# A new order for the start of an attention and expert kernel: batch 0's powers in two chains, its weight norm on TensorE, three products in two turns

## The chip, the cores and the metric

The kernel runs on one core of a Trainium2 chip. The metric is the device time of one execution in microseconds, the median of three runs.

## The reference, cut to what matters

Eight batches of Nystrom attention (8 heads, 576 positions, 64 wide, 32 landmarks) feed a layer of 8 experts, of which each token takes one.

```
q_lm, k_lm = means of q, k over 18 positions each        # 32 landmarks
A  = sm(q, k_lm); Bm = sm(q_lm, k_lm); C = sm(q_lm, k)   # softmax of scaled scores
Z  = Bm.T / (norm1(Bm) * norminf(Bm) + 1e-06)            # both norms over the whole batch and head
for _ in range(6): Z = 2 * Z - Z @ Bm @ Z
x  = A @ Z @ C @ v                                       # (B*S, 512)
expert = argmax(normed x @ normed emb.T / tau)
out    = gate * (relu(x @ w1[expert]) @ w2[expert])
```

## The kernel before

Tokens of one batch mostly go to one expert, so the kernel guesses an expert per batch (`guess`, `choose`), loads that expert's two weight matrices, and computes the batch with them. A count of wrong guesses at the end decides whether a general path runs; it does not here.

One batch goes through these generators. `sums` adds the landmark means of k and q (VectorE alone, or GpSimd halves first and VectorE adds the rest). `inverse` makes Bm, its transpose bt, the two norms, and the first residual (tile ek). `powers` does the six Newton steps as powers of the residual: every step multiplies the residual with itself and with the running product, both in one group of matmuls, copies the square and adds the product. `values` takes the scores of landmark queries with all keys, `shifted` and `turned` make their softmax and transpose it (ct), and `weighted` sums the values with it (u). `landmarks` multiplies powers and u (w), transposes that (wt), takes its norm, and prepares the routing weights. `queries` and `scored` make the softmax of all queries against the landmark keys (ae, at, ab). `first_scale` takes the norm of the first expert weights, `first_weights` multiplies wt into them, `scaled` splits the scaled product into two half-precision parts (ww). `first` is the hidden layer (`ab` times `ww`, then `hidden`), `second` the output layer (`w2c` times `ht`, c a chunk of 128 tokens).

All generators are interleaved at build time by `Weave.run`. It reads three tables of characters: TURNS names the generator that takes the next turn, CHOICES picks the engine where a generator offers two, and BANKS the PSUM banks. So the order of the instructions on each engine is fixed in these tables, and each engine works through its list in that order. WARM says before which turn, and how many, 128-column filler matmuls of ones (`keep_warm`) go into TensorE's list.

For batch 0 the norm of the first weights is a sum of squares on ScalarE (L1284), the product with u is transposed on TensorE (L1031), and squared and summed on VectorE (L1040, L1042). The lines that matter in the profile: L587 fillers, L507 all matmuls of the helper `mm`, L858 transposes of ec, L667 landmark sums, L664 and L942 GpSimd's shares, L715 to L757 the norms, L996 to L1000 the powers, L1346 ww, L1385 and L1387 w2c, L1395 and L1397 ht.

Of the kernel before, what the change touches and what calls it, by code (L numbers as in the profile page):

```python
# [19 lines left out]
P = 128  # L20
# [36 lines left out]
    "0c07072o0c0i35073c07073c08073c3d002o003c00080909003d0101010101360101013600003600363g3601363h00340d34340134010d"  # L57
    "34340d34013h3h3g0d0j0j340i0o3n341j1j1j1j1j1j1j1k1j3g013h013g013j3h3g373v3u01010101013i013u0j3i013w3w3w3w3w3w3w"
    "3i3u3w3w3w3v3i3u1l1k1k1k1k3v3w3v1k3u1k0e3w3i3u3w3v3w1l3w001l1k3w3v3u0e0f0f3v3w3w3u3v1l3w3w3w3w3u3u3u3w38383v1l"
    "3v3u1l1n381l3v383k381n1l381l3v3u3838383k383v1n381l383k1n1l1m441m3j1m46461n44461m4547442n2n2n483k3l1n1n3o3m0j45"  # L60
    "1n4702381n3m1n3m3m021n02023m382n2n3m2n382n1n023m1n2n2n38384a024b4c1n2n3l384d49022n2n4e2n4a4b3m2n4f2n482n4g4c49"
    "024d2n4h024e3o0p0p1n4f1n4h4g3l3o1n2n4j1n1n022n4k4k1n2n2o3o4m020o4n4j2n4u2o3m1o1p1o1o1o1o1o1o1p3o022o1o3o4v4v4m"
    "4m1n4v024u4l1p4v024v4m3l4m024l2n4x1n491n2o1p022n4y4i02391p4x024w382o022n39024y022o02501n2o39501q4z4w504z2o3939"
    "1q49030303033p545550035003032o1p4w0303500p54551q032o501q1s2o552o1p504i2o551q1q2o4w031s544o4i03030350032o501q1p"
    "1s5003502o2o54032o4w032o0u540p03501q50031q3a54035054505003541q552o505455551s552o2o3a2o2o2o3a2o592o1s50540k2o1s"
    "55543a593a2o3a502o5559553a3b1s1s5a5a5a505054552o5a1s503q3q3q5a3b3b5a2o3q552o3b1s5a3b5d5d5d1s3q0u5a2o5d3q5d3q5a"
    "5d5a5d5d5a5d5d2o5a3q0k0l5d58583q522o3q542o5a5a3q1s1s1q1s5a3q2o3q5a5a5a525a1s1s585m1r5o5n3b2o5a5n2o525b5b1s3q2o"
    "2o2o2o2o2o2o1s2o2q5o5a1s3q5a1s5n2p2p5a2p2p5o5m3q1s5s5q4o0v2p5b5p5q2p0l5p2p1s2p0v5t5s2q4o5u1s5m4o5t2p5z2p2q5p5w"
    "4o4o605u2p623b5z2p2p5y5w631s2p645y62605y602p5y63613q1061605f2p640404045x615x655y652q603r3r3r3r2q5x04102p6d6d04"
# [400 lines left out]
def nystrom_moe(ctx: ExitStack, tc: tile.TileContext, qT, kT, v, emb, w1, w2, out):  # L470
# [86 lines left out]
    invw = cst.tile([P, B], F32, name="invw")  # L557

    ge = cst.tile([P, B], F32, name="ge")
    gi = cst.tile([P, B], I32, name="gi")  # L560
# [1022 lines left out]
```

## Time and profile before

| | us |
|---|---|
| median of 3 runs | 425.93 |
| lowest, highest | 424.93, 426.79 |
| profiled execution, its own time | 424.86 |
| its span | 423.1 |
| TensorE, VectorE, ScalarE, GpSimd busy | 408.1, 323.5, 258.4, 72.2 |

The span is what the profile shows of one execution; 1.8 us of its time lie around it. In the rows an instruction has its start, its length, its line, and what goes out and in; in brackets stands how long the engine was idle before it, and what it waited for. Lengths of neighbours overlap a little, so the distance between two starts is what an instruction takes up.

### The profile page before, as it was taken

The numbers are of one execution on the slowest core, as the hardware profiler recorded it, in microseconds if no ns is written. First come the engines' busy times: TensorE is split into PE (matmuls) and PEld (weight loads), VectorE is DVE, ScalarE is ACT, GpSimd is POOL, SyncE is SP. The second block draws the span as 40 slices with busy tenths as digits, with TensorE's granted clock in tenths as the row PEclk, the third lists the DMA queues.
The fourth block names the chain that finished last, engine by engine and source line by source line (L and its number), as shares of the span: only waits on it lengthen the run. The fifth ranks groups of instructions, "written<-read, shape, count | busy, mean of one in ns | idle before, by whom it ended". The sixth has DMA issues, their size and how long they took to land.

```text
span 423.1 us, 14672 instructions
## 1 busy us (share of the span) xinstructions
PE 408.1 (96%) x6109; PEld 246.5 (58%) x6109; DVE 323.5 (76%) x1018; ACT 258.4 (61%) x564; POOL 72.2 (17%) x72
## 2 busy tenths in 40 slices
PE   7998999999999999999899999999999999999995
PEld 2543665566644567555575476556665576457644
DVE  4888898989799599986994889947994687668400
ACT  1367579567636985675379747963559548774211
POOL 4133213401233103301222013010320010000000
PEclk9999799999999999999999999999999999999999
DMA  8996079026368937944657239503078218321011
GB/s 298 394 398 210 2 276 384 30 77 203 119 214 309 379 120 238 341 162 142 226 155 288 108 142 359 193 29 107 16 238 324 96 44 319 109 107 51 15 64 57
DMA packets 29850, 77.68 MB, mean 184 GB/s; under 512 B 2768, under 2 KB 14288, under 8 KB 27984
## 3 DMA queue, kind: packets, MB, share of 16 engines
q1 hardware_dynamic: 29488, 76.49, 51.1%
q8 instruction: 49, 0.80, 0.8%
q10 hardware_dynamic: 288, 0.18, 0.2%
q14 instruction: 25, 0.20, 0.2%
HBM read 61.92 MB, written 14.75 MB: 181 GB/s over the span
## 4 chain that ended last, share of the span: by engine, by line
PE 76%; DVE 15%; ACT 5%; issue 2%; DMA 1%; SPq 0%; ACTq 0%; DVEq 0%
PE ps L507 71%; PE ps L587 3%; DVE ht L1397 3%; DVE w2c L1387 2%; DMA q_t<-qT 1%; PE ps L858 1%; ACT junk L1284 1%; DVE qsum L667 1%; DVE cm L804 1%; DVE ae L908 1%; ACT junk L1156 1%; ACT junk L1360 1%; DVE am L915 1%; DVE at L927 1%; DVE asum L921 1%
## 5 line engine op out<-in xcount | busy, mean ns | idle before, releaser
L507 PE MATMUL ps<-w2c,ht 128*128 128x512 f16 (+2 forms) x1176 | 203.6, 341 | 0.6 <-DVE yt L1486 0.6
L507 PEld LDWEIGHTS <-ht 128*128 128x128 f16 (+1 forms) x1176 | 93.2, 102 | 76.5 <-issue 4.5
L507 PE MATMUL ps<-ab,ww 128*128 128x288 f16 x768 | 105.0, 291 | 2.2 <-DVE ww L1346 1.0
L507 PEld LDWEIGHTS <-ww 128*128 128x128 f16 x768 | 74.9, 100 | 30.9 <-issue 4.7
L1395 ACT ACTIVATE ht<-ps 128x288 f16<-128x288 f32 x128 | 50.6, 409 | 53.7 <-PE ps L507 53.0
L1397 DVE SCALAR_TENSOR_TENSOR ht<-ps,ht 128x288 f16<-128x288 f32 x128 | 54.7, 446 | 7.6 <-ACT ht L1395 7.2
L1387 DVE SCALAR_TENSOR_TENSOR w2c<-wstage,wsc,w2c 128x1024 f16<-128x1024 f32 x32 | 41.9, 1309 | 3.4 <-ACT w2c L1385 3.3
L1488 ACT ACTIVATE yt<-ps,gfac 128x512 f32<-128x512 f32 (+1 forms) x34 | 21.5, 634 | 33.3 <-PE ps L507 31.3
L1284 ACT ACTIVATE junk<-wstage 128x1024 bf16<-128x1024 f32 x32 | 33.8, 1056 | 3.4 <-DMA wstage<-w 2.9
L1360 ACT ACTIVATE junk<-wstage 128x1024 bf16<-128x1024 f32 x32 | 33.8, 1055 | 0.7
L1156 ACT ACTIVATE junk<-ps 128x512 bf16<-128x512 f32 (+1 forms) x40 | 23.8, 596 | 15.3 <-DVE lg L1153 13.0
L942 POOL TENSOR_TENSOR ae<-ae,am 128x576 f32<-128x576 f32 x15 | 18.2, 1221 | 77.5 <-DVE am L915 57.8
L1174 POOL TENSOR_TENSOR nrm<-ssq,half 128x5 f32<-128x5 f32 x8 | 9.7, 1208 | 109.9 <-ACT junk L1156 109.9
L587 PE MATMUL ps<-ones 128*128 128x512 bf16 (+3 forms) x90 | 24.2, 405 | 1.7 <-POOL ones L525 1.7
L1153 DVE TENSOR_REDUCE lg<-ps 128x8 f32<-128x64 f32 (+1 forms) x40 | 8.8, 220 | 18.1 <-ACT junk L1156 10.9
L1385 ACT ACTIVATE w2c<-wstage,wsc 128x1024 f16<-128x1024 f32 x19 | 21.7, 1143 | 1.3 <-PE ps L507 1.3
L1346 DVE SCALAR_TENSOR_TENSOR ww<-ps,wsc,ww 128x1024 f16<-128x1024 f32 (+1 forms) x18 | 20.6, 1159 | 1.6 <-ACT ww L1344 1.5
L664 POOL TENSOR_TENSOR half<-k_t 128x576 f32<-128x576 f32 x10 | 13.0, 1297 | 46.7 <-DMA k_t<-kT 24.1
L942 POOL TENSOR_TENSOR ae<-ae,asum 128x576 f32<-128x576 f32 x12 | 13.9, 1160 | 38.2 <-DVE asum L780 24.2
L664 POOL TENSOR_TENSOR half<-q_t 128x576 f32<-128x576 f32 x10 | 14.0, 1404 | 34.2 <-DMA q_t<-qT 15.3
L507 PEld LDWEIGHTS ps<-ek 32*32 32x32 f32 x768 | 12.0, 104 | 12.6 <-DVE ek L1000 4.0
L507 PE MATMUL ps<-ek 32*32 32x64 f32 (+1 forms) x768 | 17.6, 214 | 1.4 <-issue 0.7
(209 smaller groups left out, 524.1 us busy)
## 6 DMA issues: line engine op xcount, KB each, us to landing
wstage<-w SPq DMA_DIRECT2D x64, 512.0 KB, 8.0
v<-v SPq DMA_DIRECT2D x16, 512.0 KB, 7.4
k_t<-kT SPq DMA_DIRECT2D x7, 1152.0 KB, 6.6
q_t<-qT SPq DMA_DIRECT2D x7, 1152.0 KB, 6.6
out<-yt SPq DMA_DIRECT2D x31, 256.0 KB, 3.9
abs__127<-ab SPq DMA_DIRECT2D x8, 576.0 KB, 5.3
k_t<-kT SPq DMA_DIRECT2D x2, 576.0 KB, 4.1
q_t<-qT SPq DMA_DIRECT2D x2, 576.0 KB, 6.6
```

Of the source, the lines that this page charges most:

```text
L507: pe.matmul(o, lhsT, rhs, start=start, stop=stop)
L587: pe.matmul(warmth[:, 0:k * P], ones16, bc(ones16.unsqueeze(1), [P, k, P]), start=True, stop=True)
L664: pool.tensor_tensor(out=half, in0=sv[:, :, :, 0:9], in1=sv[:, :, :, 9:18], op=ALU.add)
L942: pool.tensor_tensor(out=x, in0=x, in1=z, op=op)
L1156: act.activation(junk[lo:hi, 0:512].rearrange("p (j g x) -> p j g x", j=4, g=2), pfv[lo:hi, :, n, :, 0:D], AF.Square, accum_out=ssq[lo:hi, ...
L1284: act.activation(junk, stage[1, b, q], AF.Square, accum_out=sq[:, q:q + 1])
L1360: act.activation(junk, stage[2, b, q], AF.Abs, accum_out=sq[:, q:q + 1])
L1385: act.activation(w[:, 0], st, AF.Copy, scale=sc)
L1387: vec.scalar_tensor_tensor(out=w[:, 1], in0=st, scalar=sc, in1=w[:, 0], op0=ALU.mult, op1=ALU.subtract)
L1395: act.activation(ht[:, 0, r], ph[:, 0:HS], AF.Relu)
L1397: vec.scalar_tensor_tensor(out=ht[:, 1, r], in0=ph[:, 0:HS], scalar=0.0, in1=ht[:, 0, r], op0=ALU.max, op1=ALU.subtract)
L1488: act.activation(yt[:, 0:n], py[:, cols], AF.Copy, scale=fac)
```

## The change

1. `first_scale` for batch 0 multiplies each 128-column block of the weights (their upper halves, read as bf16) with itself on TensorE, adds all 32 products in one bank, and takes the diagonal by one fused VectorE instruction.
2. `powers` for batch 0 becomes two generators: `squares` (TensorE, then one copy) and `products` (TensorE, then one addition on VectorE), so that the squares do not wait for the additions.
3. `landmarks` for batch 0 gets the transposed product by a second group of matmuls instead of a transpose; its norm is one fused VectorE instruction on the transposed tile (`bound`).
4. `values`, `queries` and `weighted` are two turns each, and of `values` each half's maximum may start when its half is done.
5. `inverse`: the larger row sum is the product of the softmax sum and its reciprocal, and the sign of the residual is carried into the first addition. The scale of the first weights is made of the bits of both norms at once, with one reciprocal.
6. `second_weights` may take its sums on VectorE.
7. Small tiles have more buffers, and TURNS, CHOICES, BANKS and WARM are new. The description of the change says of the new order that GpSimd may hold VectorE up in it.

```
 TURNS, CHOICES, BANKS: new strings
-WARM = {18: 69, 26: 35, 47: 9, 52: 28, 60: 2, 89: 20, 103: 30, 107: 12, ... 204: 3}      # 18 entries
+WARM = {17: 53, 22: 68, 27: 3, 32: 10, 50: 8, 52: 1, 66: 1, 77: 9, ... 203: 11, 208: 13} # 20 entries
 def inverse(bs):
-        vec.tensor_reduce(ntv[:, 1], bm, axis=AX.X, op=ALU.add, apply_absolute_value=True)
+        vec.tensor_tensor(out=ntv[:, 1], in0=bs4, in1=br4, op=ALU.mult)
...
-        wv.add(powers(bs, t))
+        if bs == (0,):
+            ts = [t]
+            wv.add(squares(ts))
+            wv.add(products(ts))
+        else:
+            wv.add(powers(bs, t))
+    def squares(ts):
+        for k in range(5):
+            pz, done = yield from take(T(170, 32, cols=64, tiles="blocks"), 1)
...
+                    mm(pzv[r, g], ts[k][r, 0, 1, g], ts[k][r, 0, 1, g])
+            yield "get", "ek"
+            ts.append(residual(1))
...
+            if (yield "any", (("act", 115), ("dve", 135))) == "act":
+                act.copy(ts[k + 1][:, 0, 1], pzv)
...
+    def products(ts):
+        for k in range(6):
+            if k:
+                yield "wait", ("r", k)
...
+                    mm(pzv[r, g], ts[k][r, 0, 1, g], ts[k][r, 0, 0, g])
...
+            vec.tensor_tensor(out=ts[k + 1][:, 0, 0], in0=ts[k][:, 0, 0], in1=pzv, op=ALU.add if k else ALU.subtract)
+    def bound(b, sq, *tiles):
+        if b == 0:
+            vec.tensor_tensor_reduce(ws2, *tiles, *tiles, 1.0, 1e-30, ALU.mult, ALU.add, sq)
+            pf, put = yield from take(T(130, 4, cols=4), 1)
+            f2 = pf[:, 0:1]
+            mm(f2, ones, sq)
+        else:
+            f2, put = yield from total(sq, 1)
+        vec.tensor_scalar(hbw[:, b:b + 1], f2.bitcast(I32), 1, EXP_MASK, op0=ALU.logical_shift_right,
+                          op1=ALU.bitwise_and)
...
 def landmarks(b):
+        if b == 0:
+            quads[b] = yield from take(T(150, 32, cols=128, tiles="halves"), QUAD, "quad")
+            pwt = quads[b][0][:, :, 512 - M:512]
...
+                    mm(pwt[64 * g:64 * g + 64, j], u0[b][r, g], x0[b][r, g])
...
+            wv.add(bound(b, sq, wt_))
 def first_scale(b):
+        if b == 0:
+            work, pg = T(700, 16, cols=1024), None
+            for q in range(4):
...
+                lead = stage[1, b, q].bitcast(BF16).rearrange("p (x i) -> p x i", i=2)[:, :, 1]
+                for i in range(8):
+                    x = lead[:, P * i:P * i + P]
+                    mm(pg[:, 0:P], x, x, start=(q == i == 0), stop=(q == 3 and i == 7))
...
+            vec.tensor_tensor_reduce(ws3, pg[:, 0:P], ident, 1.0, 1e-30, ALU.mult, ALU.add, sq1)
...
+        yield "wait", ("hbw", b)
+        vec.tensor_scalar(sc, hbw[:, b:b + 1].bitcast(F32), 2.0 ** 58, inv1[:, b:b + 1], op0=ALU.mult, op1=ALU.mult)
         yield V(20)
-        vec.reciprocal(sc, inv1[:, b:b + 1])
-        yield "wait", ("scw", b)
-        vec.tensor_scalar(sc, sc, scw[:, b:b + 1], None, op0=ALU.mult)
+        vec.reciprocal(sc, sc)
 def second_weights(b):
-            act.activation(junk, stage[2, b, q], AF.Abs, accum_out=sq[:, q:q + 1])
+            if (yield "any", (("act", 1056), ("dve", 1135))) == "act":
+                act.activation(junk, stage[2, b, q], AF.Abs, accum_out=sq[:, q:q + 1])
+            else:
+                vec.tensor_reduce(sq[:, q:q + 1], stage[2, b, q], axis=AX.X, op=ALU.add, apply_absolute_value=True)
```

VectorE, batch 0's norms (bt is Bm's transpose, nts the sums, nm their maxima, cc their product's reciprocal). Before:

```order
L735 TENSOR_REDUCE nts_116<-bt 128x2
L738 STREAM_TRANSPOSE ntt<-nts_116 128x64
L741 TENSOR_REDUCE nm<-ntt 128x2
L667 TENSOR_REDUCE ksum<-k_t 128x64
L744 TENSOR_SCALAR cc<-nm 128x1
L746 RECIPROCAL cc<-cc 128x1
L749 TENSOR_SCALAR ccb<-cc 128x32
```

and now:

```order
L741 STREAM_TRANSPOSE ntt<-nts_117 128x64
L744 TENSOR_REDUCE nm<-ntt 128x2
L747 TENSOR_SCALAR cc<-nm 128x1
L615 RECIPROCAL con<-con 128x1
L749 RECIPROCAL cc<-cc 128x1
L752 COPY ccb<-cc 128x32
```

The landmark sum of the next batch's keys (ksum) no longer stands inside the norms.

VectorE, batch 0's six additions of the powers (ek). Now, from the first to the last, with all that stands between them:

```order
L929 TENSOR_REDUCE am<-ae 128x18
L1030 TENSOR_TENSOR ek<-ek,ps 128x64
L669 TENSOR_REDUCE qsum<-half 128x64
L842 TENSOR_TENSOR cfac<-cfac,rct 128x2
L958 TENSOR_TENSOR ae<-ae,am 128x576
L935 TENSOR_REDUCE asum<-ae 128x18
L669 TENSOR_REDUCE ksum<-k_t 128x64
L783 TENSOR_SCALAR asum<-asum 128x18
L785 RECIPROCAL asum<-asum 128x18
```

This list leaves out repeats: the additions stand behind each am, behind the ae, behind the small L783 of each asum, and behind a second qsum. Before, four of the five copies of the square stood in this engine's list too, each right ahead of its addition:

```order
L998 COPY ek<-ps 128x64
L1000 TENSOR_TENSOR ek<-ps,ek 128x64
L915 TENSOR_REDUCE am<-ae 128x18
L944 TENSOR_TENSOR ae<-ae,am 128x576
L921 TENSOR_REDUCE asum<-ae 128x18
```

All five copies are ScalarE's now.

TensorE, from batch 0's last power to its weight products (ones is the filler, ws a norm's column, wt the transposed product). Before:

```order
L507 MATMUL ps<-ek 32x32 x8
L587 MATMUL ps<-ones_90 128x512
L507 MATMUL ps<-u,ek 32x64 x8
L507 MATMUL ps<-ws_600,ones_90 128x1
L1031 MATMUL ps<-ident,ws__594 128x128
L507 MATMUL ps<-ws_623,ones_90 128x1
L507 MATMUL ps<-wstage,wt 32x256 x8
```

and now:

```order
L508 MATMUL ps<-wstage 128x128
L508 MATMUL ps<-ek 32x32 x8
L508 MATMUL ps<-ek,u 64x32 x8
L508 MATMUL ps<-wstage,wt 32x256 x8
L508 MATMUL ps<-u,ek 32x64 x8
L508 MATMUL ps<-wsqw,ones 128x1
L508 MATMUL ps<-wsq_134,ones 128x1
L508 MATMUL ps<-con,wt 32x8 x8
```

Repeats and fillers are left out. The squares of the weights (wstage 128x128) stand in four groups of eight between the last three groups of powers and behind the transposed product, one group of weight products stands ahead of the norm's sum, and no filler stands between the last values' sums and the first weight product. Before, 6.5, 1.75 and 10 fillers' worth of 512 columns stood there.

## Rows read from the trace of the kernel before

**Rows 1.** The page, busy time of each engine with its share of the span and its instructions.

```profile
PE 408.1 (96%) x6109; PEld 246.5 (58%) x6109; DVE 323.5 (76%) x1018; ACT 258.4 (61%) x564; POOL 72.2 (17%) x72
```

**Rows 2.** TensorE by stretches: from and to (us), length, busy time and matmuls, granted clock as a share of the full 2.4 GHz, busy share of the DMA engines, GB/s.

```profile
24.00:38.00 14.00, 13.29 (x261) 1.00 1.03 372
38.00:41.40 3.40, 1.75 (x33) 1.00 0.09 35
41.50:48.30 6.80, 6.30 (x61) 0.51 0.00 1
50.00:410.00 360.00, 355.68 (x5475) 1.00 0.50 175
```

**Rows 3.** The page, costliest groups: line, engine, operation, tiles and shapes, count, then busy time, mean ns of one, and idle time before them.

```profile
L1387 DVE SCALAR_TENSOR_TENSOR w2c<-wstage,wsc,w2c 128x1024 f16<-128x1024 f32 x32 | 41.9, 1309 | 3.4 <-ACT w2c L1385 3.3
...
L587 PE MATMUL ps<-ones 128*128 128x512 bf16 (+3 forms) x90 | 24.2, 405 | 1.7 <-POOL ones L525 1.7
...
L664 POOL TENSOR_TENSOR half<-q_t 128x576 f32<-128x576 f32 x10 | 14.0, 1404 | 34.2 <-DMA q_t<-qT 15.3
```

**Rows 4.** TensorE's timeline: start, length (us), line, operation, tiles, count of merged instructions, idle time before them.

```profile
13.61 0.64 PE L507 MATMUL ps<-ones,v 128*128 128x1 bf16 x20
...
20.13 1.79 PE L587 MATMUL ps<-ones 128*128 128x512 bf16 x8
21.86 0.42 PE L507 MATMUL ps<-ek 32*32 32x64 f32 x16
...
31.70 0.43 PE L507 MATMUL ps<-u,ek 32*32 32x64 f32 x16
...
34.96 0.66 PE L507 MATMUL ps<-wstage,wt 64*32 64x256 f32 x16
...
38.77 0.42 PE L507 MATMUL ps<-ab,ww 128*128 128x288 f16 x2 [0.57 <-ACT ww L1344]
40.22 0.66 PE L507 MATMUL ps<-ab,ww 128*128 128x288 f16 x4 [1.03 <-DVE ww L1346]
...
51.60 1.23 PE L507 MATMUL ps<-k_t,qsum 64*32 64x288 f32 x32
...
54.97 0.81 PE L507 MATMUL ps<-w2c,ht 128*128 128x512 f16 x3
...
97.46 3.11 PE L507 MATMUL ps<-ab,ww 128*128 128x288 f16 x24
100.41 0.81 PE L507 MATMUL ps<-w2c,ht 128*128 128x512 f16 x3
```

**Rows 5.** VectorE's timeline, same columns.

```profile
15.90 0.23 DVE L721 STREAM_TRANSPOSE bt<-ek 128x64 f32<-128x64 f32 x1
16.46 0.17 DVE L1115 TENSOR_REDUCE gm<-ps 128x1 f32<-128x8 f32 x1 [0.33 <-PE ps L507]
...
18.06 1.34 DVE L667 TENSOR_REDUCE ksum<-k_t 128x64 f32<-128x1152 f32 x1
19.32 0.20 DVE L744 TENSOR_SCALAR cc<-nm 128x1 f32<-128x1 f32 x1
...
20.54 0.25 DVE L757 SCALAR_TENSOR_TENSOR ek<-ps,rct,ident 128x32 f32<-128x32 f32 x1
...
23.85 0.77 DVE L908 STREAM_TRANSPOSE ae<-ps 128x576 f32<-128x576 f32 x1
24.65 0.75 DVE L915 TENSOR_REDUCE am<-ae 128x18 f32<-128x576 f32 x1
...
25.45 0.75 DVE L944 TENSOR_TENSOR ae<-ae,am 128x576 f32<-128x576 f32 x1
26.12 0.22 DVE L1000 TENSOR_TENSOR ek<-ps,ek 128x64 f32<-128x64 f32 x1
...
29.57 1.15 DVE L944 TENSOR_TENSOR ae<-ae,asum 128x576 f32<-128x576 f32 x1
...
31.46 0.18 DVE L1000 TENSOR_TENSOR ek<-ps,ek 128x64 f32<-128x64 f32 x1
...
34.25 0.28 DVE L1042 TENSOR_REDUCE wsqw<-ws 128x1 f32<-128x128 f32 x1
...
36.40 0.21 DVE L1298 TENSOR_SCALAR wsc<-wsc,scw 128x1 f32<-128x1 f32 x1
...
49.83 0.86 DVE L715 TENSOR_TENSOR ek<-be,bs 128x64 f32<-128x64 f32 x1
...
53.94 1.27 DVE L1387 SCALAR_TENSOR_TENSOR w2c<-wstage,wsc,w2c 128x1024 f16<-128x1024 f32 x1
```

**Rows 6.** ScalarE's timeline, same columns.

```profile
23.46 0.21 ACT L996 COPY ek<-ps 128x64 f32<-128x64 f32 x1 [4.62 <-DVE am L915]
23.83 1.06 ACT L1284 ACTIVATE junk<-wstage 128x1024 bf16<-128x1024 f32 x1 [0.16 <-DMA wstage<-w]
...
29.17 1.06 ACT L1284 ACTIVATE junk<-wstage 128x1024 bf16<-128x1024 f32 x1
```

**Rows 7.** GpSimd's timeline, same columns.

```profile
28.95 1.16 POOL L942 TENSOR_TENSOR ae<-ae,asum 128x576 f32<-128x576 f32 x1 [4.28 <-DVE asum L780]
...
49.32 1.29 POOL L664 TENSOR_TENSOR half<-k_t 128x576 f32<-128x576 f32 x1 [2.92 <-DVE qsum L667]
```

More of the change, by code (lines that the diff above doesn't have):

```diff
@@ L788, in values @@
         ecs = [wk.tile([P, S], F32, name="ec", bufs=BUFS["ec"]) for _ in range(2)]
-        pc, done = yield from take(T(1030, 65, cols=3200, tiles="heads"), QUAD, "quad")
+        cm = wk.tile([P, 2], F32, name="cm", bufs=3)
+        cs = wk.tile([P, 2], F32, name="cs", bufs=3)
+        neg = wk.tile([P, 2], F32, name="cneg", bufs=3)
+        work = T(515, 32, cols=1600, tiles="heads")
+        pc, done = yield from take(work, QUAD, "quad")
         pcv = pc.rearrange("p (g i) x -> p g i x", g=2)[:, :, :, 0:HS]
         for g in range(2):
+            if g:
+                yield work
             for i in range(2):
@@ L834, in weighted @@
             yield "wait", ("v", b, g)
-        pu, done = yield from take(T(1150, 161, cols=2560, tiles="columns"), 1)
+        work = T(575, 80, cols=1280, tiles="columns")
+        pu, done = yield from take(work, 1)
         for g in range(2):
+            if g:
+                yield work
             for c in range(5):
@@ L887, in queries @@
             for i in range(n):
+                if i:
+                    yield work
                 hf = n * p + i
@@ L1014, in landmarks @@
         yield "get", "wt"
-        pw, done = yield from take(T(250, 32, cols=256, tiles="blocks"), 1)
+        sq = wk.tile([P, 1], F32, name="wsqw", bufs=3)
+        wt = wts[b] = wk.tile([P, 4, M], F32, name="wt", bufs=BUFS["wt"])
+        wt_ = wt.rearrange("p j m -> p (j m)")
+        work = T(250, 32, cols=256, tiles="blocks")
+        if b == 0:
+            quads[b] = yield from take(T(150, 32, cols=128, tiles="halves"), QUAD, "quad")
+            pwt = quads[b][0][:, :, 512 - M:512]
+            for g in range(2):
+                for j in range(4):
+                    r = slice(32 * j, 32 * j + 32)
+                    mm(pwt[64 * g:64 * g + 64, j], u0[b][r, g], x0[b][r, g])
+            who = yield "any", (("act", 167), ("dve", 202))
+            (act.copy if who == "act" else vec.tensor_copy)(wt, pwt)
+            wv.flag(("wt", b))
+            wv.add(bound(b, sq, wt_))
+        pw, done = yield from take(work, 1)
         for g in range(2):
@@ L1059, in landmarks @@
             yield "wait", ("rows", b - 3)
+            yield "wait", ("saved", b - 3)
         wd = wgd[b % 3]
         yield VP(16)
-        wen = wk.tile([P, 2, E], F32, name="wen")
+        wen = wk.tile([P, 2, E], F32, name="wen", bufs=3)
         vec.tensor_scalar(wen, pg, scw[:, b:b + 1], None, op0=ALU.mult)
@@ L1308, in first_weights @@
         work = T(1880 / parts, 128 // parts, cols=16 * 1024 // parts, tiles="heads")
-        pww, done = yield from take(work, QUAD, "quad")
+        if b:
+            pww, done = yield from take(work, QUAD, "quad")
+        else:
+            pww, done = quads[b]
+            yield work
         pww = pww.rearrange("p (h g) x -> p h g x", g=2)
```

299 lines of the change are left out of this document (167 added, 132 removed).

## The prediction

> **What bounds the kernel now.** I read the busy shares first, then TensorE by stretches, then the costliest groups, then TensorE's own timeline up to the second expert layer, and only then the engines that feed it. TensorE is busy 96% of the span [rows 1]; between 50 and 410 us it idles 4.3 us in all [rows 2], so nearly every microsecond of work there is a microsecond of the kernel. What can be won is therefore in the first 55 us, and three things show there. Filler matmuls (ones times ones) take 24.2 us [rows 3], all ahead of the first expert layer. The powers start at 21.86 and the last one is added at 31.46 [rows 4, 5]. And the first expert layer, which begins at 38.77, does not flow: TensorE waits 0.57 and 1.03 us in it [rows 4], is busy only 1.75 of the 3.40 us from 38.0, and then its granted clock is 0.51, the lower of its two levels (1.2 GHz of 2.4), from 41.5 to 48.3 [rows 2]. That stretch costs 6.8 x 0.49 = 3.3 us.
>
> My mark is the start of the first matmul of batch 0's second layer, 54.97 us [rows 4]. In both programs the same 72 hidden-layer matmuls, one expert guess and 16 score matmuls stand between the first hidden-layer matmul and the mark, so whatever is earlier at the mark is earlier for all that follows, if that is kept.
>
> **To the first power.** In before, VectorE's row ksum (1.34 us) sits inside the chain of norms, from 18.06 to the start of cc at 19.32 [rows 5]; in the new order it comes later. That takes 1.26 us out. The absolute row sum of Bm becomes a product of two small tiles: 0.2 us at most. Ahead of it the transpose bt (15.90) stood behind both column maxima and seven small instructions; now two of those come behind it, the first column maximum starts as soon as half of the landmark scores are there, and TensorE has 2 instead of 7 fillers ahead: gm comes at 15.9 instead of 16.46, about 0.6 us. Norms from gm to the second ek took 16.46 to 20.79; now 15.9 + 4.33 - 1.26 - 0.2 = 18.8. In before, eight fillers then held the first power back until 21.86, 1 us after its data [rows 4, 5]. In the new TensorE order the two query turns and their shorter fillers end at about 19.1. So the first power starts **2.8 us earlier**.
>
> **The powers.** Splitting them keeps TensorE's work the same: 11 times 8 matmuls of 32 columns for 5 times 8 of 64 and 8 of 32. All five squares are copied by ScalarE (0.21 us each [rows 6]; in before VectorE made four of these five copies). What sets the end is VectorE, whose six additions now stand between long instructions: two transposes ae (0.77 long, 0.70 to the next start), two am and two asum (0.75, 0.67 to the next), one ksum (1.34, 1.28 to the next), one qsum of half a tile (0.68 by the same measure), one subtraction (0.75, and 0.4 more if GpSimd holds it as at 29.57), the additions themselves (0.13 from 26.12 on) and 0.5 of small ones: 9.2 us [rows 5]. 18.8 + 9.2 = 28.0, against 31.64: **3.6 us earlier**. The bound below is no hold and no small ones, 27.1; the bound above the pace of before, 9.8 us behind 19.1, 28.9.
>
> **From the powers to the scale.** Before: product, copy, transpose, copy, square, sum, ones-product and bits from 31.70 to 36.61, 4.9 us [rows 4, 5]. Now the transposed product is a matmul of its own: 28.0 + 0.3, ScalarE's copy to 28.6; VectorE has a ksum (1.28) and a transpose (0.70) ahead of the norm and is free at 30.1. Of its fused multiply-and-sum no row exists. The nearest is the sum of 34.25 (0.28) which it replaces together with a product of the same size [rows 5]; I take 0.45 for each of two, between 0.28 and both apart, 0.56. Ones-product 0.3, then five dependent small ones of 0.15 to 0.2: the scale stands at about 31.9, **4.7 us earlier**. The norm of the first weights leaves ScalarE (four times 1.06 us [rows 6]) for 32 matmuls of 128 columns. No row has them. The guess's 128x1 matmuls load weights of the same strided kind, 20 in 0.64 us, 0.032 each; 128 columns are a quarter of a 512-column filler, 1.79 for 8, 0.056 each [rows 4]. Columns alone are one end, 1.8 us; both in full, the other, 2.8. I take 2.8, because each has its own weights. They stand beside the additions, on a TensorE that waits there anyway. Their cover is the data: the first weights' first quarter was read at 23.83 after a wait of 0.16, the fourth at 29.17 [rows 6], and the transfers keep the DMA engines at 1.03 from 24 to 38 us [rows 2]; the fourth product, at about 28.5, may wait up to 0.7 us.
>
> **To the mark.** ScalarE scales from 32.25, behind one sum of the second weights; VectorE has a transpose (0.70), a residue (0.68) and wen (0.2) ahead of its first ww (0.66) and ends that at 34.2. TensorE meanwhile has three quarters of the weight products (0.66 each [rows 4]), three small groups and some 6 fillers behind the ones-product of 30.6, and starts the hidden layer at **35.2**. From there: 72 x 0.123 (24 in 2.95 us, 97.46 to 100.41 [rows 4]) = 8.9, scores 1.2 (51.60), guess 0.6, gr some 0.4, a wait of 0.65 for the sum of the second weights (ScalarE ends the fourth at 37.9) and 0.25 for gr: 47.2. VectorE's ht, which have 9.2 us of work between the first and the twelfth, pull it to **48.3**. 54.97 - 48.3 = 6.7 us.
>
> A second account, by TensorE's work alone: 31 fillers of 512 columns fewer, one of 384 and four of 128 more, 29 in all at 0.224 = 6.6 us less; products 2.8 more; transpose 0.3 less: 4.1. The half clock, 3.3, if it does not come again. New waits against old ones: near zero. 7.4, so 6.7 is not out of reach.
>
> **Behind the mark.** TensorE's work there is the same to within single instructions. GpSimd has 52 instead of 47 of the 576-wide instructions (1.16 to 1.40 each [rows 3, 7]); in exchange VectorE has four fewer full sums (1.34, by some 0.6 each) and eleven copies fewer, and four outputs and eight sums of second weights more, for which no row exists (ScalarE's 1.06 is the lower end, w2c's 1.31 the upper [rows 3, 6]). These nearly balance, but an ek of 0.86 instead of 0.21 and an ae of 1.15 instead of 0.75 stand in before exactly where GpSimd runs a half or an ae [rows 5, 7], so I take 0.7 us off: one such hold on the path. The span loses **6.0 us**. The profiled execution was 424.86 (span 423.1, 1.8 around it), so 418.9; it lies 1.07 under the median of the three runs, 425.93, so I predict **419.9**.
>
> **The rivals.** About 0.5%, 2.1 us, is what a measurement of this kernel can tell from no change: faster is under 423.8, slower over 428.06.
>
> *A. The lower clock comes again.* In before it fell behind 1.65 us idle of 3.40. In my sum TensorE idles about 2.7 of the 5.9 us from 24.7 to 30.6 (waiting for two additions and for the norm), with small matmuls between; fillers are gone from exactly there. Against it: over the 14 us from 24 on, with small matmuls and fillers mixed, the clock of before stayed at 1.00 [rows 2]. Price: at most 3.3, and part of it falls where TensorE waits anyway: 3.0, **422.9**. Chance 0.28.
>
> *B. The time is given back behind the mark.* Every order has its own idle slices; the old one has 4.3 us [rows 2]. VectorE and DMA then meet the same work in a shorter span, and in the new order batch 3's first hidden matmul follows its weight products by only 48 half-width matmuls and 16 small ones. If idle time doubles, 419.9 + 4.3 = **424.2**. Chance 0.12.
>
> *C. GpSimd holds VectorE, and it comes out slower.* Place: VectorE's instructions with two inputs in SBUF (ab, ek, w2c, ae) that the new order lets fall beside GpSimd's 52. Price: 0.65 each (0.86 - 0.21, the free one's size by the addition at 26.12 [rows 5]). To be slower by 0.5% 13 of them have to be on the path that TensorE waits for: 419.9 + 13 x 0.65 = **428.4**. For it: the nearest row of before is such a hold at 49.83, in the hidden layer. Against it: w2c, the longest of these, averages 1.31 where the one at 53.94, beside no GpSimd row, took 1.27 [rows 3, 5], so holds are few; and TensorE waits for VectorE at most 4.3 us behind the mark. Chance 0.08. [...]
>
> *D.* That the new order's chain is not what sets the end (the weights land later) is inside the range: 0.7 us above.
>
> **How the numbers follow.** Forecast 0.52. Faster: nearly all of it, 0.72 of A, a quarter of B: 0.74. Same: the rest of A, most of B, little of the forecast: 0.17. Slower: C and what I have not seen: 0.09. Below, the range takes in the hold that doesn't come (0.7), the mark at 47.2 (1.1) and a third of the idle slices (1.3): 416.8. Above it takes in A and B: 424.4.
>
> **What would show it.** First power near 19.1, last addition near 28, VectorE's wsc near 31.8, first hidden matmul near 35.2, first second-layer matmul near 48.3; ht twelve times without a gap; a granted clock of 1.00 from 24 to 50; idle slices behind 50 of about 4 us together. Wrong if the mark is earlier by 6 us and the end is not: then it was B or C, told apart by VectorE's mean ek, ae and w2c. Wrong in the mark itself if the clock is 0.5 between 28 and 40 (A), or if the first hidden matmul is past 37 at full clock: then the fused sums or the landing of the weights were priced too low.

## The result, and the profile after

The change makes the kernel slightly slower: 427.52 us median (425.31 to 430.48, 20 runs) against 425.35 (424.05 to 426.79, 20 runs), a ratio of 1.0053 [1.0033, 1.0072]. 419.9 us was forecast, faster. The profiled execution of after took 428.5 us (span 426.7).

| step (us) | before | forecast | after | light3 |
|---|---|---|---|---|
| first power | 21.86 | 19.1 | 20.23 | 19.86 |
| last addition of the powers ends | 31.64 | 28.0 | 32.93 | 28.38 |
| first hidden-layer matmul | 38.77 | 35.2 | 40.79 | 35.97 |
| first second-layer matmul (the mark) | 54.97 | 48.3 | 56.35 | 50.21 |

(light3 is an experiment below: after with most of batch 0's weights not loaded. The columns are single executions; that of after took 1.0 us more than its median, that of light3 1.6 less, so they lie further apart than the medians do.) The busy times barely differ from [rows 1]; nothing of what follows shows there.

```profile
PE 410.3 (96%) x6212; PEld 248.1 (58%) x6212; DVE 325.6 (76%) x1008; ACT 245.6 (58%) x551; POOL 82.8 (19%) x77
```

TensorE's timeline of after shows where the time at the start went (columns as in [rows 4]):

```profile
20.23 0.33 PE L508 MATMUL ps<-ek 32*32 32x32 f32 x16
...
24.26 0.75 PE L508 MATMUL ps<-v,ct 128*32 128x64 f32 x37
28.34 0.30 PE L508 MATMUL ps<-v,ct 128*32 128x64 f32 x3 [3.33 <-issue]
...
29.91 1.03 PE L508 MATMUL ps<-wstage 128*128 128x128 bf16 x8
...
40.79 2.37 PE L508 MATMUL ps<-ab,ww 128*128 128x288 f16 x18
...
44.66 0.16 PE L508 MATMUL ps<-ws,ones 128*128 128x1 bf16 x1 [1.03 <-DVE ws L977]
...
46.23 0.39 PE L508 MATMUL ps<-gr,ones 128*128 128x8 f32 x2 [0.65 <-DVE inv L992]
...
47.88 2.15 PE L508 MATMUL ps<-k_t,qsum 64*32 64x288 f32 x16
...
50.82 1.18 PE L508 MATMUL ps<-k_t,qsum 64*32 64x288 f32 x16
...
56.35 0.81 PE L508 MATMUL ps<-w2c,ht 128*128 128x512 f16 x3
```

Inside one group of weighted sums, between two matmuls that wait for no engine and no load, TensorE stands still for 3.33 us. "issue" says that the profile has nothing that it waited for. Before has one stop of this kind at the start, of 0.71 us, inside a power:

```profile
27.82 0.41 PE L507 MATMUL ps<-ek 32*32 32x64 f32 x10
28.94 0.31 PE L507 MATMUL ps<-ek 32*32 32x64 f32 x6 [0.71 <-issue]
```

By stretches of after (columns as in [rows 2]), the DMA engines are full while it stands, and 1.2 us after it goes on its granted clock falls to 0.50; that happens a second time behind the two waits at 44.66 and 46.23:

```profile
25.00:28.30 3.30, 0.01 (x2) 1.00 1.01 375
28.30:29.60 1.30, 1.26 (x48) 0.99 1.01 394
29.60:33.00 3.40, 3.40 (x71) 0.50 0.97 316
33.00:46.60 13.60, 11.12 (x204) 1.00 0.49 178
46.70:50.00 3.30, 3.30 (x23) 0.50 0.00 0
50.00:410.00 360.00, 356.88 (x5455) 1.00 0.50 174
```

VectorE's additions wait for the stop. Later its fused sum (L1073) and a scale of two columns (L710) stand beside GpSimd's work. Here is VectorE in after, then GpSimd:

```profile
24.61 0.21 DVE L1030 TENSOR_TENSOR ek<-ek,ps 128x64 f32<-128x64 f32 x1
...
30.04 0.22 DVE L1030 TENSOR_TENSOR ek<-ek,ps 128x64 f32<-128x64 f32 x1 [3.21 <-PE ps L508]
...
34.93 0.89 DVE L1073 CUSTOM_DVE_ANT_0 ws<-wt 128x128 f32<-128x128 f32 x1
...
35.97 0.29 DVE L1382 CUSTOM_DVE_ANT_0 ws<-ps,ident 128x128 f32<-128x128 f32 x1
...
44.58 0.90 DVE L710 TENSOR_SCALAR br<-bs 128x2 f32<-128x2 f32 x1
```

```profile
34.51 1.16 POOL L956 TENSOR_TENSOR ae<-ae,asum 128x576 f32<-128x576 f32 x1 [0.80 <-DVE asum L785]
...
43.51 1.94 POOL L666 TENSOR_TENSOR half<-q_t 128x576 f32<-128x576 f32 x1 [7.84 <-DVE ksum L669]
```

L1073 and L710 end within 0.15 us of GpSimd's instruction (35.82 and 35.67; 45.48 and 45.45). The same fused sum takes 0.25 us in paced, an experiment below, where no GpSimd instruction stands beside it (VectorE):

```profile
31.55 0.25 DVE L1095 CUSTOM_DVE_ANT_0 ws<-wt 128x128 f32<-128x128 f32 x1
```

**What the stop is.** The page lists a DMA queue of kind "instruction":

```profile
q8 instruction: 50, 0.82, 0.8%
```

These are 50 packets of 16,384 bytes. TensorE has 12,424 records in the trace (6212 matmuls and as many weight loads), some 250 to a packet. A float32 matmul leaves four of them, two matmuls and two loads: the 8 matmuls of the first power stand in after's trace, at 20.23 us, as 16 matmuls and 16 loads. Counted by records, before's stop of 0.71 us at 28.94 and after's of 3.33 at 28.34 both stand where 698 have gone, though the work there differs (a power, a weighted sum). After's second stop (1.09 us at 140.27) and before's second one (0.16) stand where 4532 and 4530 have gone: 15 times 256 further, less a few that leave no record. In all profiles of this case, every "issue" stop of 0.3 us or more stands within 14 records of such a count, which is called a boundary here. The author's estimate from these counts is that each packet brings the next 256 instructions of TensorE's program; no row shows what a packet holds. Worked out from the DMA records of the traces (us; "entered": TensorE begins the 256 instructions ahead of the boundary):

```
                     entered  packet           goes on  stop
before, 698          24.08    26.41 to 27.50   28.94    0.71
after,  698          21.91    26.00 to 26.96   28.34    3.33
after,  4532         134.16   137.78 to 138.76 140.27   1.09
shift,  954          23.39    27.21 to 28.10   29.58    2.49
defer,  954          27.02    30.85 to 31.73   33.35    2.32
```

A packet mostly takes 1.0 us (0.88 to 1.75 in before and after), and TensorE goes on 1.2 to 1.7 us after its end, at every stop over 0.3 us in the profiles of this case. Between the entry and the packet's start lies what is called its wait here. Where the DMA engines are under half busy in the 3 us behind the entry, half of the packets of before and after start at most 0.3 us after it (some 47 packets); where they are over 0.9 busy, the median is 2.8 us and the longest wait 5.7 (some 29 packets). So behind DMA engines over 0.9 busy the stops show 4.9 to 8.4 us from entry to use. Before spent 3.9 us on those 256 instructions, after 2.9, and after's packet also waited longer: 4.1 us against 2.3.

### The profile page after: what moved, and what is told of

It is laid out like the page before. It is cut to its first block, busy times and chain, and to the rows that moved or that the text cites. A ratio compares the mean times of both kernels' runs of the same rounds, so it can differ in the third digit from the quotient of the medians.

```text
span 426.7 us, 14858 instructions
## 1 busy us (share of the span) xinstructions
PE 410.3 (96%) x6212; PEld 248.1 (58%) x6212; DVE 325.6 (76%) x1008; ACT 245.6 (58%) x551; POOL 82.8 (19%) x77
## 4 chain that ended last, share of the span: by engine, by line
PE 83%; DVE 11%; issue 2%; DMA 1%; ACT 1%; POOL 0%; ACTq 0%; DVEq 0%
PE ps L508 79%; DVE ht L1510 2%; PE ps L589 2%; DVE w2c L1500 2%; PE ps L872 1%; DMA k_t<-kT 1%; DVE ww L1457 1%; DVE ksum L669 1%; DVE ab L946 1%; DVE cm L816 0%; DVE am L929 0%; DVE at L941 0%; DVE w2c L1496 0%; PE ps L873 0%; DVE ae L922 0%
## 5 line engine op out<-in xcount | busy, mean ns | idle before, releaser
L508 PE MATMUL ps<-w2c,ht 128*128 128x512 f16 (+2 forms) x1176 | 201.4, 341 | 0.6 <-DVE yt L1599 0.6
L1508 ACT ACTIVATE ht<-ps 128x288 f16<-128x288 f32 x128 | 49.7, 409 | 48.3 <-PE ps L508 46.8
L1601 ACT ACTIVATE yt<-ps,gfac 128x512 f32<-128x512 f32 (+1 forms) x30 | 18.9, 635 | 44.1 <-PE ps L508 34.9
L1242 ACT ACTIVATE junk<-ps 128x512 bf16<-128x512 f32 (+1 forms) x40 | 23.8, 595 | 17.5 <-DVE lg L1239 16.6
L1392 ACT ACTIVATE junk<-wstage 128x1024 bf16<-128x1024 f32 x28 | 29.5, 1054 | 0.5
L956 POOL TENSOR_TENSOR ae<-ae,asum 128x576 f32<-128x576 f32 x14 | 17.1, 1224 | 50.4 <-DVE cfac L837 12.6
L1498 ACT ACTIVATE w2c<-wstage,wsc 128x1024 f16<-128x1024 f32 x21 | 24.1, 1146 | 4.2 <-PE ps L508 4.2
L1471 ACT ACTIVATE junk<-wstage 128x1024 bf16<-128x1024 f32 x24 | 25.3, 1056 | 0.5
L666 POOL TENSOR_TENSOR half<-q_t 128x576 f32<-128x576 f32 x13 | 18.0, 1386 | 36.8 <-DMA q_t<-qT 23.2
L666 POOL TENSOR_TENSOR half<-k_t 128x576 f32<-128x576 f32 x11 | 15.8, 1434 | 46.9 <-DMA k_t<-kT 25.1
L589 PE MATMUL ps<-ones 128*128 128x512 bf16 (+3 forms) x64 | 17.4, 391 | 1.7 <-POOL ones L526 1.7
L1599 DVE TENSOR_SCALAR yt<-ps,gfac 128x512 f32<-128x512 f32 (+1 forms) x11 | 7.4, 675 | 15.2 <-PE ps L508 15.0
L1455 ACT ACTIVATE ww<-ps,wsc 128x1024 f16<-128x1024 f32 (+1 forms) x18 | 17.3, 1013 | 2.4 <-DVE at L941 1.3
```

Of the source, the lines that this page charges most:

```text
L508: pe.matmul(o, lhsT, rhs, start=start, stop=stop)
L589: pe.matmul(warmth[:, 0:k * P], ones16, bc(ones16.unsqueeze(1), [P, k, P]), start=True, stop=True)
L666: pool.tensor_tensor(out=half, in0=sv[:, :, :, 0:9], in1=sv[:, :, :, 9:18], op=ALU.add)
L956: pool.tensor_tensor(out=x, in0=x, in1=z, op=op)
L1242: act.activation(junk[lo:hi, 0:512].rearrange("p (j g x) -> p j g x", j=4, g=2), pfv[lo:hi, :, n, :, 0:D], AF.Square, accum_out=ssq[lo:hi, ...
L1392: act.activation(junk, stage[1, b, q], AF.Square, accum_out=sq[:, q:q + 1])
```

## The experiments

**First: is it TensorE's program?** The rival is that something which TensorE reads at that place comes late.

shift puts 102 more instructions on TensorE before 11.7 us, without a column more:

```diff
-        for i in range(0, n, 4):
-            k = min(n - i, 4)
+        step = 1 if n == 68 else 4
+        for i in range(0, n, step):
+            k = min(n - i, step)
```

> After, with the second group of early fillers issued as 68 matmuls of 128 columns in place of 17 of 512: the same columns, 102 more instructions on TensorE before 11.7 us. Theory (instruction fetch): TensorE's own program arrives in packets of 256 instructions, and it stands still where the next packet has not come; so it stops again at its 699th instruction, which is now another one, in the group of the fifth square at about 23.5 us, for 0.8 to 2.5 us, and the weighted sums at 25 us run through; 425.0 to 427.5 us (ratio 0.999 to 1.005). Rival (the place): the stop belongs to the 19th matmul of the first half of the weighted sums (something that it reads comes late); it stays there, 3.3 us long, and the time stays at 427.5 us.

It measured 430.56 us, ratio 1.0117 [1.0088, 1.0147]. The expectation was wrong in the boundary and the time, and right in that stops follow the count. The weighted sums run through (first line). The boundary at 698 costs nothing, since its packet ended at 21.2 us, ahead of its use at 23.39. The stop has gone to the next boundary, 954 records, in a power; two more end at 136.92 (0.79 us) and 143.66 (3.64 us), 4532 and 4788 records. TensorE in shift:

```profile
23.99 0.77 PE L508 MATMUL ps<-v,ct 128*32 128x64 f32 x40
...
29.58 0.26 PE L508 MATMUL ps<-ek 32*32 32x32 f32 x7 [2.49 <-issue]
```

The rival has fallen: the same matmuls run without a stop, and the stop stands 256 records further on.

light loads one sixteenth of batch 0's first weights and leaves out the rest, which is a constant (`pool.memset(st, 0.02)` at the start; the edit is condensed here, as are some of those below):

```diff
-            sp.dma_start(st, src[..., 1024 * q:1024 * q + 1024]...)
+            n = 64 if (m, b) == (1, 0) else 1024
+            sp.dma_start(st[:, 0:n], src[..., 1024 * q:1024 * q + n]...)
```

> After, with one sixteenth of batch 0's first weights loaded (the rest of those tiles is a constant, written early by GpSimd): 1.97 MB less are in flight from 19 us on. Theory (instruction fetch behind data): the packet that TensorE waits for starts within 1.5 us of the boundary ahead of it (4.09 us in after) and the stop of 3.3 us falls under 1 us; the last power addition ends before 30 us, first hidden matmul before 38 us, 420 to 424 us. Rival (the place, or an engine): less data changes nothing at 25 us, the stop stays over 2.5 us, 426.5 to 428 us. Second rival (the lower clock and the landing of weights cost most): the stop goes, but the time falls by under 1.5 us.

It measured 425.76 us, 1.0007 [0.9982, 1.0032]. The stop at 698 is 0.24 us, but stops of 0.80 and 1.68 follow at 950 and 1206, and the first power is 1.0 us later; the mark comes at 52.54 in the profiled execution, the shortest of its runs (423.45). The stop went as expected; the time is 1.8 us above the range.

defer loads everything, but issues the load of `kt[2]` behind the first piece of the second weights (in `loads` the pair goes into `late`):

```diff
             wv.flag(("w", m, b, q))
+            if b == 0 and m == 2 and q == 0:
+                sp.dma_start(*late.pop())
```

> After, with the load of batch 2's keys (1.15 MB, issued at 14.4 us ahead of the first weights, first read at 32.4 us) moved behind the first of the second weights (about 22 us). All data are loaded. Theory: fewer bytes stand ahead of the instruction packet asked for at 21.9 us; the stop falls from 3.3 to 0 to 2 us, the first weights land up to 3 us sooner, 422 to 426 us. Rival (place): the stop stays at 3.3 us and the time at 427 to 428 us.

It measured 426.69 us, 1.0026 [1.0007, 1.0044], a miss in both. The stop at 698 is still 2.44 us, and another of 2.32 us stands at 954: its packet waits 3.8 us, with the DMA engines full again.

**Second: what are the halves worth?** unsplit does the matmuls of both halves in the first of their two turns, for batches 1 to 7:

```diff
-            for i in range(2):
+            for gg in ((g,) if b == 0 else (0, 1) if g == 0 else ()):
+              for i in range(2):
```

(so in `values`, and likewise in `weighted` and `queries`)

> After, with both halves of values, queries and weighted sums of batches 1 to 7 issued in the first of their two turns (the second turn is empty). Theory: behind the first second-layer matmul, after spends 3.5 us more than before inside the groups of scores and weighted sums, because a half costs 0.05 to 0.15 us more than half of a whole group; undone, 1.5 to 2.5 us come back: 425.0 to 426.2 us (ratio 0.998 to 1.002). Rival: the longer groups are waits that would stand elsewhere, and the earlier maximum of a half was worth as much: 427 to 428.5 us.

It measured 425.62 us, 0.9989 [0.9964, 1.0014]: 2.7 us under after by the ratios, with the stop (2.92 us) still there. whole_values does it in `values` alone:

> After, with the two halves of values (landmark queries with all keys) in one turn for batches 1 to 7; queries and weighted sums stay in two. Theory: a half of values is the heads of one g, which use four of the eight tiles of the array that the whole group works on side by side, so a half takes as long as the whole (1.13 and 1.16 us); behind the first second-layer matmul this group falls from 8.91 to about 7.0 us, and most of what unsplit gave (1.9 us) comes: 425.3 to 426.5 us. Rival (queries and weighted sums cost it): 426.8 to 427.6 us.

It measured 426.26 us, 1.0014 [0.9989, 1.0040], over half of that gain. Half of values takes as long as the whole. Here are the two halves of batch 1 in light3, at the full clock; both together take 1.23 us in [rows 4]:

```profile
42.74 1.17 PE L508 MATMUL ps<-k_t,qsum 64*32 64x288 f32 x16
...
44.69 1.18 PE L508 MATMUL ps<-k_t,qsum 64*32 64x288 f32 x16
```

A half of values is one g, and by the kernel's indices the heads of one g use four of the eight 64x32 tiles that the whole group uses. In before the matmuls of the whole at 51.60 us start eight together, within 0.07 us, the eights 0.24 to 0.27 us apart; in after those of the half at 50.82 start four together, within 0.02 us, and the fours are just as far apart. So both take four such steps. A half of queries holds both g: in after it takes 0.63 us in the mean to the next instruction's start, where the whole takes 1.13. Behind the mark TensorE's steps from start to start add up, for these three kinds of groups (k_t, q_t and v,ct), to 23.8 us in before, 27.3 in after and 24.0 in unsplit; for values (k_t) alone to 7.0, 8.9 and 6.9.

**Third: without the bytes, is the new order worth what was forecast?** light2 and light2_before leave out fifteen sixteenths of batch 0's first and second weights, in after and in before, with GpSimd's memsets of the constant behind its power at 9 us:

> After, with one sixteenth of batch 0's first and second weights loaded (the rest of the eight tiles is a constant that GpSimd writes behind its first power at 9 us): 3.9 MB less in flight from 19 us on. Theory (the data ahead of TensorE's instruction packets): each packet asked for between 22 and 36 us starts within 1 us, no stop over 0.5 us is left there, and after gets the lead that was forecast of it: 1.5 to 5 us less than light2_before. Rival (the new order itself is worth nothing: the halves of values, the holds and the lower clock take what the two chains give): the same within 1 us as light2_before.

> Before, with the same sixteenth of batch 0's weights. Theory: its stop at the 698th instruction was 0.7 us, so lighter data give it little: 0 to 1.5 us under before (ratio 0.996 to 1.000). Rival (landing of the weights bounds the start of both kernels): over 2 us under before.

They measured 428.46 us (1.0065 [1.0035, 1.0095]) and 433.39 (1.0174 [1.0141, 1.0207]). The times of this pair say nothing of the bytes: VectorE was held beside the memsets, and the first power came at 25.44 and 29.98 us. In light2, GpSimd, then VectorE:

```profile
11.41 7.21 POOL L608 MEMSET wstage<- 128x1024 f32 x8
```

```profile
14.57 4.08 DVE L714 TENSOR_SCALAR br<-bs 128x2 f32<-128x2 f32 x1
```

No stop over 0.15 us is left at the start in either, as expected of the bytes. light3 and light3_before have ScalarE write the constants instead, at the start:

```diff
+    for m in (1, 2):
+        for q in range(4):
+            st = stage[m, 0, q] = wst.tile([P, 1024], F32, tag=f"st{m}", ...)
+            act.activation(st..., bc(ones...), AF.Copy, scale=0.02)
...
-            sp.dma_start(st, src[..., 1024 * q:1024 * q + 1024]...)
+            n = 64 if b == 0 else 1024
+            sp.dma_start(st[:, 0:n], src[..., 1024 * q:1024 * q + n]...)
```

> After, with one sixteenth of batch 0's first and second weights loaded, the rest of the eight tiles written as a constant by ScalarE in its first 10 us (by GpSimd, in light2, VectorE was held for 4 us ahead of the first power). Theory (TensorE's instruction packets behind data): first power at about 20.2 us as in after, no stop over 0.5 us between 20 and 36 us, last addition ended by 29.5 us, first second-layer matmul at 49 to 51.5 us; 420 to 423.5 us (ratio 0.988 to 0.995) and 1.5 to 5 us under light3_before. Rival (the new order is worth nothing by itself: from first power to first second-layer matmul light2 took 31.98 us, light2_before 31.39): the same within 1 us as light3_before.

> Before, with the same sixteenth of batch 0's weights and ScalarE's constants. Theory: its stop of 0.7 us goes and little else: 423.5 to 425.5 us (ratio 0.995 to 1.000). Rival (the landing of the weights bounds the start): under 422.5 us.

They measured 423.61 us (0.9962 [0.9945, 0.9979]) and 424.00 (0.9970 [0.9951, 0.9988]). The start of light3 goes as the theory says: one stop of 0.40 us, full clock to 419 us, the last addition 0.4 and the first hidden matmul 0.8 us from the forecast. Taking the bytes away is worth 3.9 us to after and 1.3 to before. It takes away all that hangs on these bytes, the landing of the weights too, so the 3.9 us are not the stops alone. At the end the two are equal, and the rival that called the new order worthless by itself is not refuted by this pair. TensorE in light3:

```profile
23.89 1.09 PE L508 MATMUL ps<-v,ct 128*32 128x64 f32 x40
...
29.19 0.30 PE L508 MATMUL ps<-ek,u 32*64 32x32 f32 x4 [0.40 <-issue]
```

light3_unsplit joins the two edits:

> light3 with the halves of values, queries and weighted sums of batches 1 to 7 in one turn. Theory (the halves cost what unsplit gave, and that adds to the stops): 1.3 to 2.2 us under light3, 421.4 to 422.3 us (ratio 0.990 to 0.993); the first second-layer matmul 1.0 us sooner (batch 1's values cost 1.17 in place of 2.27 us), behind it 0.3 to 1 us less. Rival (both take from the same slack): 423 to 423.8 us.

It measured 421.16 us, 0.9890 [0.9866, 0.9915]: 0.72% under light3, 3.1 us, and 0.8% under light3_before. So without those bytes and without the halves the new order is worth 0.8%. (The mark did not come sooner as expected: 51.66 us in the profiled execution, the longest of its runs, with two stretches at the lower clock.) light3_rest takes the two waits behind the first hidden matmul away as well (`n = 64 if b == 0 and q > 1 else 1024` columns in two of the four sums of the second weights; two of GpSimd's landmark halves on VectorE):

> light3_unsplit, with the last two of the four sums of batch 0's second weights over 64 of 1024 columns (the rest is left out), and two of GpSimd's landmark halves (batch 2, first of q, second of k) on VectorE. Theory: the waits of 1.29 and 0.65 us go, VectorE's two-column scale is no longer held (0.15 in place of 0.90 us), the first second-layer matmul stands at 47 to 48.5 us (48.3 was forecast of the change) and the whole at 419.5 to 421.3 us (419.9 was forecast). Rival (something else behind the first hidden matmul bounds it): over 421.5 us.

It measured 421.00 us, 0.9895 [0.9866, 0.9923]: no further. The waits are gone, VectorE's scale takes 0.17 us, and the mark stands at 49.47; three stops of TensorE's program, of 0.62 to 0.94 us, stand at the start of this profile instead. What the waits cost was not measurable here.

**What can be had with all data.** nohold moves one landmark half from GpSimd to VectorE:

```diff
+                if (b, nm, x) != (2, "q", 0):
                     pool.tensor_tensor(out=half, ...)
```

> After, with the first landmark sum of batch 2's queries on VectorE alone, where its turn for the second part stood (GpSimd's 1.94 us at 43.51 us goes, VectorE's 0.74 us becomes 1.34 us). Theory: VectorE's two-column scale at 44.58 us takes 0.15 us in place of 0.90, and TensorE's wait of 0.65 us for the norm of the second weights at 46.23 us goes: 426.5 to 427.2 us (ratio 1.002 to 1.004). Rival (the wait has another cause, or is given back behind it): 427.2 to 427.8 us.

It measured 426.50 us, 1.0027 [1.0001, 1.0052], inside the range, but not for the reason expected: GpSimd's next half (k_t, 43.59 us, 1.94 long) took the place of the one removed, VectorE's scale still took 0.91 us and TensorE's wait 0.66. Its interval overlaps after's; nothing follows from the time. combo joins unsplit with nohold and defer:

> After with three edits together: halves in one turn for batches 1 to 7, batch 2's keys loaded behind the first of the second weights, batch 2's first query sum on VectorE. If the three add up as measured or forecast alone (1.9, 0.8 and 0.6 us), 424.2 us, within 423.0 to 425.2 (ratio 0.994 to 0.999). If the stops of TensorE's program only move, as with the shifted boundary, 425.2 to 427 us.

It measured 425.42 us, 1.0005 [0.9982, 1.0027], with stops of 2.84, 0.79 and 0.96 us by 41 us: they only move. unsplit_held2 is unsplit with two landmark halves moved to VectorE (`HELD = (2, "q", 0), (2, "k", 1)`):

> After with all data loaded, halves in one turn for batches 1 to 7 and the same two landmark halves on VectorE. Theory: unsplit's 425.6 us less the wait of 0.65 us: 424.5 to 425.3 us, ratio 0.996 to 0.999, still with the stop of about 3 us at 25 us. Rival (nothing gained behind the stop): 425.4 to 426.2 us.

It measured 424.40 us, 0.9982 [0.9960, 1.0003]. VectorE's scale takes 0.17 us and TensorE's wait is gone; stops of 3.57 and 1.36 us remain by 43 us. It is the fastest version with all data; that it beats before is not shown. paced holds SyncE back by a one-element DMA that reads the third piece of w1, and adds shift, unsplit, nohold, defer and 38 tiny matmuls:

> After with all data loaded and five edits: halves in one turn for batches 1 to 7; batch 2's first query sum on VectorE; batch 2's keys behind the first of the second weights; SyncE holds the second weights back until the third piece of the first has landed; the 102 early instructions of the shifted boundary, and 152 more (38 tiny matmuls) where TensorE waits at 44 us, so that the packets' boundaries behind that stand where they stood in after. Theory: the packets asked for at 19.4, 23.4 and 26.9 us start within 2 us, the stops of 20 to 36 us fall from 3.3 to under 1.5 us, 421.5 to 424.5 us (ratio 0.990 to 0.998). Rival (data that start later land later, and what waits for them gives the gain back): 425 to 427 us.

It measured 426.45 us, 1.0029 [1.0015, 1.0043]. It does not compute what the reference does, and why is open, so only its trace is read. The stops at the start fall to one of 0.82 us, and that is given back: the scale of the first weights stands at 34.42 us (37.53 in after) but the first hidden matmul at 40.19, behind a wait of 1.33 us and with 6.8 us of lower clock from 30.1. Last in this group comes after once more, beside these versions:

> After, unchanged, beside the others on one chip: 426.5 to 428 us (ratio 1.002 to 1.007), its stop at the 698th instruction between 2.5 and 4.5 us long.

It measured 427.78 us, 1.0061 [1.0036, 1.0087], with a stop of 2.84 us.

**Last: instructions alone.** before_more is before with 160 more instructions for the same columns; before_more_al adds 96 more at 41 us, so that the later boundaries fall where before has them:

```diff
-                        mm(pzv[r, i, 0:a, g], t[r, i, 1, g], t[r, i, 0:a, g])
+                        for x in ((slice(0, 1), slice(1, 2)) if bs == (0,) and a == 2 else (slice(0, a),)):
+                            mm(pzv[r, i, x, g], t[r, i, 1, g], t[r, i, x, g])
```

> Before, with each of batch 0's first five power groups issued as 16 matmuls of 32 columns in place of 8 of 64: the same columns and results, 160 more instructions on TensorE between 22 and 29 us, no other edit. Theory (instructions, not columns, run out): the 699th instruction now stands in the weighted sums at about 25.7 us, the 256 ahead of it last 3.2 us in place of 4.2, and the stop there grows from 0.7 to between 1.2 and 3.5 us; behind 50 us the boundaries move by 160 and stops there may change by up to 4 us either way; 426.5 to 431 us (ratio 1.002 to 1.013). Rival (instruction count is free, order and waits made the stop): no stop over 1 us before 36 us, 425 to 426.3 us.

> The same, with 96 more instructions (24 tiny matmuls) ahead of the norm of batch 0's second weights at 41 us, so that all boundaries behind that fall where before has them. Theory: the stop at the start as in before_more (1.2 to 3.5 us), behind 50 us the stops of before (0.2 us in all); with up to 1 us for the tiny matmuls 426.5 to 429.5 us (ratio 1.002 to 1.009). Rival: 425 to 426.5 us.

They measured 436.46 us (1.0269 [1.0253, 1.0286]), 5 us above the range, and 428.88 (1.0088 [1.0067, 1.0110]), inside it. TensorE in before_more_al:

```profile
24.67 1.19 PE L507 MATMUL ps<-v,ct 128*32 128x64 f32 x66
28.30 0.42 PE L507 MATMUL ps<-v,ct 128*32 128x64 f32 x14 [2.44 <-issue]
```

Before gets a stop like after's, in the same weighted sums, and becomes 3.9 us slower, from 160 instructions without a column more and the 96 tiny ones at 41 us (what the 96 cost by themselves was not run; up to 1 us was expected). Without the 96, the shifted boundaries cost before_more another 7.6 us: it has six stops, 9.2 us in all, the longest 3.71 us up to 234.74, at 7340 records.

## Why the prediction was wrong, point by point

- **"Splitting them keeps TensorE's work the same"** is the step that failed first. In columns it does; in instructions it is 11 groups of 32 for 6 of 32. The 256 that follow the 442nd record went by in 2.9 us instead of 3.9, and the next packet ended at 26.96 us, after they had gone by: a stop of 3.33 us instead of 0.71. before_more_al shows that instructions alone do this to before (2.44 us of stop, 3.9 us of time); light3 shows the stop at 698 away with the bytes. The lower clock of 29.6 to 33.0 came with the stop. In nine of the eleven profiles with a stop of over 2 us at the start the clock fell between 0.7 us before and 1.3 us after TensorE went on (in defer it fell later, in before_more_al not until 44.55, so such a stop alone does not do it); in light, light3 and light3_rest, whose stops by 40 us are 0.24 to 1.68 us, it did not fall before 418 us. The prediction had "issue" in its trace, 0.71 us at 28.94, and did not ask what it was.
- **"The same ... 16 score matmuls stand between the first hidden-layer matmul and the mark", scores 1.2 us, and "TensorE's work there is the same to within single instructions"** failed too. The counts hold, the time does not, since values are cut by g. It cost 2.7 us (unsplit) to 3.1 us (light3_unsplit).
- **The first power** came 1.1 us later than forecast. Its data stood at 19.56 us, not 18.8, and TensorE's second query turn and a filler ended at about 20.2, not 19.1. gm came at 16.79, not 15.9: between the end of the second maximum (15.10) and gr (16.10) nine small instructions stand in VectorE's list, where before has four. This was read, not run; light3 has it as well (19.86).
- **The powers** came out right in size, in part by luck. From first power to last addition 8.9 us were forecast; light3 took 8.5, after 12.7. But the terms of the forecast's sum, as listed, add up to 8.5 us and not to 9.2. light3 spent 9.2 us from the second ek to the last addition, with a second qsum (0.66) and a wait for TensorE (0.68) that the sum does not name, and without the hold of 0.4.
- **The fused sums** were taken at 0.45 us each: 0.25 to 0.29 with no GpSimd instruction beside them, 0.89 for the first beside one. The squares of the weights, 2.8 us forecast, took 0.63 per eight at the full clock, 2.5.
- **Rival A** (lower clock) came, 3.4 us twice, behind the stop and behind two waits; before had 6.8 in one, so nothing was won or lost by it in sum, where the forecast won 3.3. What the two levels cost is in the hidden layer of before: its 288-column matmuls follow one another every 0.240 us at 0.50 and every 0.122 at 1.00. **Rival C** (GpSimd holds VectorE) came at two places at the start, 0.6 and 0.75 us, and not at 13; light3_rest, without the second, is no faster. Of the means that the prediction named as its sign, ae fell from 0.85 to 0.76 us, the ek of the norms from 0.38 to 0.21, and w2c rose from 1.31 to 1.33. Both of the held ones, L1073 and L710, ended within 0.15 us of GpSimd's instruction. The prediction looked for C at instructions with two inputs in SBUF; that others are spared is not shown: L710 has one, and took 0.90 us at 44.58 and 0.16 at 15.02, where GpSimd did nothing. **B** came, by the halves and not by idle slices (3.7 us behind the mark, 4.9 before).
- By the ratios, in per cent of before: forecast -1.4, measured +0.5. Taking the bytes away gives 0.9 (after less light3), the halves 0.7 (light3 less light3_unsplit), each within some 0.3; together 1.6 of the 1.9. For the last 0.3, 1.3 us, no run isolates a cause; the late first power is a candidate. Taking the bytes away also helps before by 0.3, so of the 0.9 the change itself answers for 0.6.

## What to carry to other kernels

Count instructions, not only columns, where small float32 matmuls are put close together while the DMA engines are full. TensorE stood still here where 256 of its instructions went by in less time than lay between a packet's entry and its use, 4.9 to 8.4 us at the stops behind DMA engines over 0.9 busy. Behind less busy ones it was shorter, but not nothing: at a stop of light3_rest, with the DMA engines 0.15 busy, 3.7 us. The "issue" stops of 0.3 us and more, in the middle of groups of matmuls, stood within 14 records of a boundary in every profile here. Instructions added far ahead moved them: 102 early ones put shift's stop at 954 instead of 698, and the 160 of before_more, without the 96 of before_more_al, cost 7.6 us behind them. So a small edit can change the time for reasons far from it. And before cutting a group of tiled matmuls in two, look which tiles of the array each part uses: a part on half of the tiles took as long as the whole here (1.17 and 1.23 us).

## What was not expected of the hardware

- TensorE stops with nothing in the profile that it waits for, in after for 3.33 us with the DMA engines 1.01 busy: 47 stops of 0.3 us and more in 18 profiles, each ending 1.2 to 1.7 us behind the end of a packet of 16,384 bytes.
- VectorE's scale of two columns took 4.08 us in light2, beside GpSimd's memsets of 0.9 us each, and ended within 0.1 us of the last of them: it was held over several short instructions of GpSimd in a row, not over one. The same scale took 0.16 us in after at 15.02, with no GpSimd instruction beside it.
- SyncE was caught by the stop too: in after its reload of v, which overwrites what the weighted sums read, was issued at 28.68 us, and the last two second weights behind it from 29.35, against 22.32 in before. What that cost was not tried.
